# Attention, low-rank mixing and a split FFN on one core: tiles of 384 tokens from batch 2 on, short transfer latencies in the planned order, and batch 1 computed the early way

## Chip, cores and metric

The kernel runs on one core of a Trainium2 chip. The metric is the device time of one launch in microseconds (us). The core has five engines that run side by side, each taking its own instructions in order: TensorE (PE, with the loading of weights shown apart as PEld), VectorE (DVE), ScalarE (ACT), GpSimd (POOL) and SyncE (SP), which here issues the transfers between memory and on-chip buffers (DMAs).

## What is computed

There are 8 batches of 576 tokens and 8 heads of 64 channels. Each head adds two attentions: one over sequences pooled by four (144 tokens, its result repeated four times) and one over a band of seven neighbouring tokens. The result x (576 x 512 per batch) is mixed along the sequence by a product of rank 32, and then goes through an FFN of 512 to 2048 to 512 with a ReLU and a residual.

```python
q_d = q.reshape(B, H, Sd, factor, D).mean(axis=3)        # factor 4, k_d and v_d alike
out_up = np.repeat(sm_attn(q_d, k_d, v_d), factor, axis=2)
mask = np.abs(pos[:, None] - pos[None, :]) < factor
scores = np.where(mask, scale * np.matmul(q, k.transpose(0, 1, 3, 2)), -1e9)
x = out_up + np.matmul(softmax(scores), v)               # then (B, S, H * D)
h = xt @ U @ V                                           # xt: x with tokens last, rank 32
u = x + h.transpose(0, 2, 1)
return u + np.maximum(u @ w_ch1, 0.0) @ w_ch2
```

## The kernel before

**The FFN.** Tokens are cut into 16 tiles of 288, two per batch. A tile takes 16 steps, one for each 128 of the 2048 hidden channels, so there are 256 steps. A step is `ffn1` (12 matmuls at L902 into one bank `ps_h`) and, three steps later (LAG), `ffn2` (12 matmuls at L926 into four banks `acc`). The products are made of three matmuls each, since every operand is split into a high and a low part: uH and uL, hH and hL, and the two parts of the weights W. Between the two, ACT makes hH (L910) and DVE hL (L911) from `ps_h`. Up to step 19 (H1) `ps_h` has only one bank for `ffn1`, as the other serves the conversion of the weights, which arrive in 64 bits and are split by ACT, DVE and POOL (`convert`, its last piece on POOL at L357). After the last step of a tile POOL (L937) and DVE (L940) add u, and the tile is stored.

**The attention** goes by pairs of heads, four pairs per batch, numbered 0 to 31 here. It has two ways. The early way (pairs below NE = 4, batch 0) stays on the chip: banded scores in blocks on PE (L601), their transposes (L644) and products (L656), the pooled attention (ps_s L459, ps_t L488, ps_a L499), transposes of the outcome (L678, L679, L685), and the mixing by U (ps_hu, L697 and L699). POOL pools q and k (L428, L430) and v (L445, L448). The late way (all other pairs) makes band scores on PE (L745, L751, L758), bounces them and the results through memory (s_s, up_s, x_s), computes the band on POOL (L829), DVE (L834) and ACT, and mixes with ps_hu at L878 from xH and xL (L870 on POOL). Both ways end in `u_tail`: ps_u at L715, the sum on DVE, uH on ACT (L722), uL on POOL (L724). An FFN tile needs uH and uL of all four pairs of its batch.

**The order.** Nothing is issued in the order of the source. Every operation goes into a `Plan` with its engine, a cost, what it reads and writes and a priority; `Plan.run` is a list scheduler that lets the five engines run in modelled time and takes on each the ready operation of lowest priority value. Attention has priorities from 0 to 319 (10 per pair), the weights 30 and up, FFN steps 1000 and up, so FFN matmuls fill what attention leaves free, and the outcome is a fixed order of instructions for each engine. A matmul of the FFN costs PH or PF in the plan. A transfer costs its bytes plus a latency, and late transfers (priority from 50, and again from 80) a surcharge of 1.5 to 4 us (L262), so their readers are put later in the order. The buffers of the late way are opened (`open_late`) when all early work is done. Attention of batch b + 1 enters the plan with the first step of batch b.

Of the kernel before, what the change touches and what calls it, by code (L numbers as in the profile page):

```python
# [200 lines left out]
def attn_mix_ffn_kernel(ctx: ExitStack, tc, q, kp, vp, qT, kT, v, U, Ub, V, w1, w2, edge, band, eye, pool, vw, ident, outT):  # L201
# [507 lines left out]
    def u_tail(b, hp, stk, lt, xT, bank, prio):  # L709
        for t in range(NT):  # L710
            tsl = slice(t * TN, (t + 1) * TN)
# [2 lines left out]
            def um(tsl=tsl, pu=pu):
                nc.tensor.matmul(pu()[:, :TN], lt(), Vst[:, tsl], start=True, stop=True)  # L715
            op(PE, 0.14, um, [(stk, 0), (stk, 1), (stk, 2), "V0H", "V1H", "V0L", "V1L"], [pu], prio)
# [2 lines left out]
            dve(TN, lambda pu=pu, uf=uf: nc.vector.tensor_tensor(
                out=uf(), in0=pu()[:, :TN], in1=uf(), op=ALU.add), [pu, ufk], [ufk], prio)  # L720
            uH, uL = u_of(b, t)
            act(TN, lambda uH=uH, uf=uf: nc.scalar.activation(uH()[:, hp, :], uf(), AF.Copy),  # L722
                [ufk], [(uH, hp)], prio, 0.1)
            pool_tt(TN, lambda uH=uH, uL=uL, uf=uf: nc.gpsimd.tensor_tensor(  # L724
                out=uL()[:, hp, :], in0=uf(), in1=uH()[:, hp, :].bitcast(F32), op=ALU.subtract),
                [ufk, (uH, hp)], [(uL, hp)], prio)
# [114 lines left out]
    def u_of(b, t):
        if (b, t) not in u_bufs:
            u_bufs[(b, t)] = (buf(ffn, [128, NDC, TN], F32R, "uH", bufs=2), buf(ffn, [128, NDC, TN], F32R, "uL", bufs=2))
        return u_bufs[(b, t)]
# [211 lines left out]
```

## Time and profile before

| what | us |
|---|---|
| median of 3 runs (lowest, highest) | 1018.7 (1018.46, 1018.81) |
| the profiled execution | 1018.72 |
| its span, first to last instruction | 1016.9 |
| first FFN matmul starts | 62.56 |
| last piece of FFN matmuls ends | 1012.11 |

The span is what the profiler saw of the core; the 1.8 us around it belong to the launch. Busy time is given by engine; a PE that is busy has an instruction in it, at whichever clock was granted. A row of the timeline gives the start, the length, the engine, the line, the tile written and those read, the shapes (contraction x weight columns, then output partitions x columns), how many instructions are drawn together, and in brackets the idle time ahead of them with what ended it. Lengths of neighbouring matmuls overlap, so what one costs is read from start to start. Rows of POOL are rough.

### The profile page before, as it was taken

The numbers are of one execution on the slowest core, as the hardware profiler recorded it, in microseconds if no ns is written. First come the engines' busy times: TensorE is split into PE (matmuls) and PEld (weight loads), VectorE is DVE, ScalarE is ACT, GpSimd is POOL, SyncE is SP. The second block draws the span as 40 slices with busy tenths as digits, with TensorE's granted clock in tenths as the row PEclk, the third lists the DMA queues.
The fourth block names the chain that finished last, engine by engine and source line by source line (L and its number), as shares of the span: only waits on it lengthen the run. The fifth ranks groups of instructions, "written<-read, shape, count | busy, mean of one in ns | idle before, by whom it ended". The sixth has DMA issues, their size and how long they took to land.

```text
span 1016.9 us, 26970 instructions
## 1 busy us (share of the span) xinstructions
PE 981.1 (96%) x10820; PEld 962.4 (95%) x10820; DVE 471.1 (46%) x945; ACT 387.5 (38%) x1239; POOL 578.6 (57%) x651
## 2 busy tenths in 40 slices
PE   5889899999999999999999999999999999999998
PEld 4679789989999999999999999999999999999998
DVE  5788864534544445454443445445443344221111
ACT  4866644433343342443443333333433232111110
POOL 6667897867565557675756657476675543211010
PEclk9979999999999999999999999999999999999999
DMA  9677955646364465564455553446555241000000
GB/s 262 196 233 210 278 132 125 169 100 148 81 148 106 120 134 138 119 142 106 106 144 123 139 122 92 114 101 159 132 130 122 65 99 53 8 6 19 6 20 24
DMA packets 222981, 120.23 MB, mean 118 GB/s; under 512 B 174772, under 2 KB 199176, under 8 KB 222856
## 3 DMA queue, kind: packets, MB, share of 16 engines
q1 hardware_dynamic: 222856, 118.51, 46.2%
q8 instruction: 85, 1.39, 0.6%
q14 instruction: 40, 0.33, 0.1%
HBM read 87.60 MB, written 30.86 MB: 116 GB/s over the span
## 4 chain that ended last, share of the span: by engine, by line
PE 87%; DMA 3%; POOL 3%; ACT 3%; DVE 2%; issue 1%; SPq 1%; POOLq 0%; ACTq 0%; DVEq 0%
PE ps_h L902 37%; PE acc L926 37%; PE ps_a L564 3%; PE ps_b L745 2%; PE ps_hu L878 2%; PE ps_t L551 1%; DMA vr<-in_v 1%; PE ps_b L758 1%; DMA gT<-in_kT 1%; POOL Pt L829 1%; PE ps_u L715 1%; POOL W L357 1%; PE ps_a L499 1%; DMA wr<-in_W 0%; DMA xL<-x_s 0%
## 5 line engine op out<-in xcount | busy, mean ns | idle before, releaser
L926 PE MATMUL acc<-hH,W 128*128 128x288 f32 x2048 | 463.1, 299 | 3.0 <-POOL W L357 3.0
L902 PE MATMUL ps_h<-uH,W 128*128 128x288 f32 x2048 | 455.5, 297 | 6.3 <-DVE hL L911 5.9
L902 PEld LDWEIGHTS ps_h<-uH,W 128*128 128x128 f32 x2048 | 345.6, 189 | 8.3 <-DVE hL L911 7.4
L926 PEld LDWEIGHTS acc<-hH,W 128*128 128x128 f32 x2048 | 344.3, 188 | 5.1 <-POOL W L357 4.1
L902 PE MATMUL ps_h<-uL,W 128*128 128x288 f32 x1024 | 304.0, 297 | 2.2 <-POOL uL L724 2.2
L911 DVE SCALAR_TENSOR_TENSOR hL<-ps_h,hH 128x288 fp32r<-128x288 f32 x256 | 116.7, 456 | 400.6 <-ACT hH L910 400.0
L926 PE MATMUL acc<-hL,W 128*128 128x288 f32 x1024 | 301.2, 294 | 0.0
L829 POOL TENSOR_TENSOR Pt<-vl,at 128x896 f32<-128x896 f32 (+1 forms) x140 | 242.5, 1808 | 56.4 <-DVE acc L834 49.9
L910 ACT ACTIVATE hH<-ps_h 128x288 fp32r<-128x288 f32 x256 | 105.1, 410 | 440.2 <-PE ps_h L902 440.1
L902 PEld LDWEIGHTS ps_h<-uL,W 128*128 128x128 f32 x1024 | 193.9, 189 | 2.4 <-POOL uL L724 2.4
L926 PEld LDWEIGHTS acc<-hL,W 128*128 128x128 f32 x1024 | 192.9, 188 | 0.0
L834 DVE TENSOR_REDUCE acc<-Pt 128x128 f32<-128x1024 f32 (+1 forms) x140 | 150.9, 1104 | 9.4 <-POOL Pt L829 4.8
L870 POOL TENSOR_TENSOR xL<-xL,xH 116x640 fp32r<-116x640 f32 x28 | 44.0, 1571 | 91.5 <-ACT xH L869 82.0
L724 POOL TENSOR_TENSOR uL<-xT,uH 128x288 fp32r<-128x288 f32 x64 | 50.2, 808 | 70.2 <-ACT uH L722 70.1
L937 POOL TENSOR_TENSOR o<-uH,uL 128x288 f32<-128x288 f32 x64 | 49.7, 811 | 55.1 <-DMA out_t<-o 55.1
L776 ACT ACTIVATE se<-ps_b 96x114 f32<-96x114 f32 x112 | 40.0, 357 | 57.1 <-PE ps_b L751 35.6
L823 ACT ACTIVATE Pt<-ul 128x128 f32<-128x128 f32 (+1 forms) x140 | 49.8, 442 | 21.6 <-DVE acc L834 17.6
L522 POOL TENSOR_TENSOR vr<-vr 72x256 f32<-72x256 f32 x56 | 41.4, 740 | 23.7 <-DMA vr<-in_v 23.7
L357 POOL TENSOR_TENSOR W<-c,W 128x512 fp32r<-128x512 f32 x32 | 41.3, 1292 | 13.1 <-ACT W L354 12.8
L537 ACT ACTIVATE E<-ps_b,nb 72x144 f32<-72x144 f32 x112 | 40.9, 373 | 0.6
L532 DVE TENSOR_REDUCE mx<-ps_b 72x2 f32<-72x288 f32 x56 | 23.1, 448 | 35.4 <-ACT se L776 32.9
L940 DVE TENSOR_TENSOR o<-acc,o 128x288 f32<-128x288 f32 x64 | 26.6, 452 | 24.3 <-PE acc L926 21.9
(134 smaller groups left out, 894.6 us busy)
## 6 DMA issues: line engine op xcount, KB each, us to landing
wr<-in_W SPq DMA_DIRECT2D x32, 512.0 KB
vl<-in_vp SPq DMA_DIRECT2D x56, 240.0 KB
vr<-in_v SPq DMA_DIRECT2D x64, 144.0 KB
out_t<-o SPq DMA_DIRECT2D x64, 144.0 KB
gT<-in_kT SPq DMA_DIRECT2D x28, 291.0 KB
gq<-in_qT SPq DMA_DIRECT2D x28, 288.0 KB
up_s<-od SPq DMA_DIRECT2D x112, 72.0 KB
ul<-up_s SPq DMA_DIRECT2D x28, 288.0 KB
```

What stands on the lines that cost most here:

```text
L357: pool_tt(1.0 * n, lambda: nc.gpsimd.tensor_tensor(out=lo_out(), in0=ta()[l0:], in1=hi_out()[l0:].bitcast(F32), op=ALU.subtract), [t, *own ...
L522: pool_tt(256, lambda x=x: nc.gpsimd.tensor_tensor(out=x()[:, :, 0:2, :], in0=x()[:, :, 0:2, :], in1=x()[:, :, 2:4, :], op=ALU.add), [x], ...
L724: pool_tt(TN, lambda uH=uH, uL=uL, uf=uf: nc.gpsimd.tensor_tensor(out=uL()[:, hp, :], in0=uf(), in1=uH()[:, hp, :].bitcast(F32), op=ALU.su ...
L823: act(n * D, lambda n=n, ps=ps, Pt=Pt: nc.scalar.activation(Pt()[:, :n, :, 7], ul()[:, ps, :], AF.Copy), [ul], [(Pt, 1)], prio, 0.16)
L829: nc.gpsimd.tensor_tensor(out=Pt()[:, :n, :, 0:7].rearrange("p s d o -> p o s d"), in0=win, in1=at()[:, ps, :].rearrange("p s o -> p o s") ...
L834: dve(8.5 * n * D, lambda n=n, ps=ps, Pt=Pt: nc.vector.tensor_reduce(out=acc()[:, ps, :], in_=Pt()[:, :n], axis=AX.X, op=ALU.add), [(Pt, 0 ...
L870: pool_tt(640, lambda: nc.gpsimd.tensor_tensor(out=xL(), in0=xL().bitcast(F32), in1=xH().bitcast(F32), op=ALU.subtract), [xL, xH], [xL], prio)
L902: nc.tensor.matmul(ps()[:, :TN], W1[fc]()[:, w, dc, :], u()[:, dc, :], start=(n == 0), stop=(n == 3 * NDC - 1))
L910: last_h[i] = act(TN, lambda: nc.scalar.activation(hH(), ps()[:, :TN], AF.Relu), [ps], [hH], FIRST, 0.05)
L911: dve(TN, lambda: nc.vector.scalar_tensor_tensor(hL(), ps()[:, :TN], 0.0, hH().bitcast(F32), op0=ALU.max, op1=ALU.subtract), [ps, hH], [hL ...
L926: nc.tensor.matmul(ac[e]()[:, :TN], W2[fc]()[:, w, es], hx(), start=(fc == 0 and n == 0), stop=(fc == NFC - 1 and n == 2))
L937: pool_tt(TN, lambda e=e, o1=o1: nc.gpsimd.tensor_tensor(out=o1()[:, :TN], in0=uH()[:, e, :].bitcast(F32), in1=uL()[:, e, :].bitcast(F32), ...
```

## The change

1. **Tiles.** The first two batches keep tiles of 288 tokens; the other six batches, 3456 tokens, are cut into 9 tiles of 384, which cross borders of batches. A list `tiles` holds start and width, `segs` for every batch which part of which tile it fills, and `u_tail` writes one part after the other. There are 13 tiles and 208 steps. uH and uL of a wide tile lie in two buffers (a class `Half`: three of four groups of channels together, the fourth in a ring `u3`). The sum at the end of a tile uses one buffer `o`, which shares its slot with the conversion's scratch.
2. **Early way for batch 1.** NE goes from 4 to 8, so pairs 4 to 7 go the early way and enter the plan ahead of the weights. v of these pairs is loaded and pooled head by head (two smaller sums on POOL per head).
3. **Order.** The surcharge on late transfers falls to 0.25 us from priority 50 and 0.5 from 80. PE's cost in the plan follows the width. U for the late way (`load_u`) is loaded between the weights.
4. **Room.** Pt has two buffers instead of three, od two instead of three, at is written over ms, xH and Y share a slot.

```diff
-    TN = 288
+    TN, TW = 288, 384
...
-    PH, PF = 1.587, 0.398
+    PE_N = lambda n, k: k * (n / 2400.0 + 0.0125)
...
+    UC = 10
...
-    NE = 4
-    NOD = 3
+    NE = 8
+    NOD = 2
...
-        late = (3.0 if r else 4.0) * (0.5 * (prio >= 50) + 0.5 * (prio >= 80))
+        late = 0.25 * (prio >= 50) + 0.25 * (prio >= 80)
...
-        x = (buf(early_pool, [QH, 2, 2, 4, D], F32, "vr") if b else
-             buf(wts, [QH, 2, 2, 4, D], F32, "vr", f"W2_{NFC - 6 - hp}:vr"))
...
+        both = None if b else buf(wts, [QH, 2, 2, 4, D], F32, "vr", f"W2_{NFC - 6 - hp}:vr")
+        for hh in range(2):
+            x = both or buf(early_pool, [QH, 2, 4, D], F32, "vr")
...
+            pool_tt(256, lambda xh=xh: nc.gpsimd.tensor_tensor(
+                out=xh()[:, :, 0:2, :], in0=xh()[:, :, 0:2, :], in1=xh()[:, :, 2:4, :], op=ALU.add),
+                [(x, hh)], [(x, hh)], prio)
+            pool_tt(128, lambda hh=hh, xh=xh: nc.gpsimd.tensor_tensor(
...
-        ms, mx = lb([128, NPOS, 7], "ms"), lb([128, NPOS], "lmx")
+        ms, mx = lb([128, NPOS, 7], "ms", bufs=2), lb([128, NPOS], "lmx")
...
-        at = lb([128, NPOS, 7], "at", bufs=2)
+        at = ms
...
-            Pt = buf(loc, [128, 2, D, 8], F32, "Pt", "Pt", 3)
+            Pt = buf(loc, [128, 2, D, 8], F32, "Pt", "Pt", 2)
...
+    tiles, segs = [], {}
+    for g0 in (*range(0, NB * S, TN), *range(NB * S, B * S, TW)):
+        n = TN if g0 < NB * S else TW
+        for b in range(g0 // S, (g0 + n - 1) // S + 1):
+            lo, hi = max(g0, b * S), min(g0 + n, (b + 1) * S)
+            segs.setdefault(b, []).append((len(tiles), slice(lo - b * S, hi - b * S), slice(lo - g0, hi - g0)))
+        tiles.append((g0, n))
...
-        xH = buf(mix, [MP, 2, MJ, D], F32R, "xH")
+        xH = buf(mix, [MP, 2, MJ, D], F32R, "xH", "xH:x")
...
-        Y = buf(mix, [128, S // 32, 32], F32, "Y")
+        Y = buf(mix, [128, S // 32, 32], F32, "Y", "xH:y")
...
-                    nc.tensor.matmul(ps()[:, :TN], W1[fc]()[:, w, dc, :], u()[:, dc, :],
+                    nc.tensor.matmul(ps()[:, :tn], W1[fc]()[:, w, dc, :], u.ap(dc),
...
-        mm_op[i] = op(PE, PH, mm, ur + [(W1[fc], "H"), (W1[fc], "L")], [ps], FILL + i,
+        mm_op[i] = op(PE, PE_N(tn, 3 * NDC), mm, ur + [(W1[fc], "H"), (W1[fc], "L")], [ps], FILL + i,
...
-    steps = [(b, t, fc) for b in range(B) for t in range(NT) for fc in range(NFC)]
+    steps = [(ti, fc) for ti in range(len(tiles)) for fc in range(NFC)]
...
     attention(0)
+    attention(1)
     early_ops = [o for o in plan.ops if o not in tails]
...
+        if c == UC:
+            load_u(W1P + WS * (2 * c - 1))
...
-    load_u(36)
...
-    attention(1)
+    opener = {segs[b][0][0] * NFC: b + 1 for b in range(1, B - 1)}
     for i in range(len(steps) + LAG):
         if i < len(steps):
-            b, t, fc = steps[i]
-            if t == 0 and fc == 0 and b > 0 and b + 1 < B:
-                attention(b + 1)
+            if i in opener:
+                attention(opener[i])
             ffn1(steps[i], i)
```

What this does to the order shows at three places. In the rows, L numbers are lines of the program before or after it; L902 and L926 became L939 and L964, L715 became L721, L724 became L730.

PE, the last pair ahead of the first FFN matmul (W_0 and W_1 are the first hidden chunks' weights); before:

```order
L678 MATMUL ps_c<-ident_sb,od_e_105 128x72 x2
L679 MATMUL ps_c<-ident_sb,ob 128x64
L685 MATMUL ps_x<-ident_sb,ob 128x128 x4
L697 MATMUL ps_hu<-ob,Ublk 64x128 x5
L699 MATMUL ps_hu<-od_e_105,Upool 64x128 x2
L715 MATMUL ps_u<-Vst,stk 128x288 x2
L902 MATMUL ps_h<-uH,W_0_409 128x288
L902 MATMUL ps_h<-uL,W_0_409 128x288
```

and now:

```order
L685 MATMUL ps_c<-ident_sb,ob 128x64
L691 MATMUL ps_x<-ident_sb,ob 128x128 x4
L703 MATMUL ps_hu<-ob,Ublk 64x128 x5
L705 MATMUL ps_hu<-od_e_106,Upool 64x128 x2
L494 MATMUL ps_t<-ident_sb,E_e_95 72x72 x4
L721 MATMUL ps_u<-Vst,stk 128x288 x2
L505 MATMUL ps_a<-vs_e_91,E_e_95 72x64 x4
L494 MATMUL ps_t<-ident_sb,E_e_96 72x72 x4
L505 MATMUL ps_a<-vs_e_91,E_e_96 72x64 x4
L939 MATMUL ps_h<-uH,W_0_406 128x288
L939 MATMUL ps_h<-uL,W_0_406 128x288
```

The second ps_t, ps_a, ps_t and ps_a are those of pair 4, batch 1; one ps_s of it stands a few rows further ahead. After the first two steps come the band scores; before, those of late pairs:

```order
L926 MATMUL acc_1225<-hH,W_0_959 128x288
L926 MATMUL acc_1225<-hL,W_0_959 128x288
L926 MATMUL acc_1225<-hH,W_0_959 128x288
L758 MATMUL ps_b<-smk,smq 32x144 x4
L758 MATMUL ps_b<-smk,smq 8x144 x2
L745 MATMUL ps_b<-gT,gq 32x38 x8
L751 LDWEIGHTS edge
L751 MATMUL ps_b<-edge 32x38
```

and now those of an early pair, whose 36 block matmuls (L607, L601 before) stand together:

```order
L964 MATMUL acc_1268<-hH,W_0_995 128x288
L964 MATMUL acc_1268<-hL,W_0_995 128x288
L964 MATMUL acc_1268<-hH,W_0_995 128x288
L619 LDWEIGHTS eye_sb
L619 MATMUL ps_b<-band_sb,eye_sb 128x190
L619 LDWEIGHTS eye_sb
L619 MATMUL ps_b<-band_sb,eye_sb 128x190
L607 MATMUL ps_b<-kd,qt 32x38 x36
L939 MATMUL ps_h<-uH,W_2_607 128x288
```

PE at the start of tile 2, the first of batch 1 (W_0 again, step 32); before, the end of step 31, the mixing of pair 7 and its ps_u stand directly ahead of it:

```order
L926 MATMUL acc_2486<-hH,W_15_2383 128x288
L926 MATMUL acc_2486<-hL,W_15_2383 128x288
L926 MATMUL acc_2486<-hH,W_15_2383 128x288
L878 MATMUL ps_hu<-xH,Ust 64x128 x5
L878 MATMUL ps_hu<-xL,Ust 64x128 x5
L715 MATMUL ps_u<-Vst,stk 128x288 x2
L902 MATMUL ps_h<-uH,W_0_409 128x288
L902 MATMUL ps_h<-uL,W_0_409 128x288
L902 MATMUL ps_h<-uH,W_0_409 128x288 x2
```

and now the last ps_hu and ps_u of pair 7 stand around the `ffn1` of step 29 (W_13), and step 30 (W_14) and others follow ahead of step 32:

```order
L964 MATMUL acc_2391<-hH,W_10_1899 128x288
L703 MATMUL ps_hu<-ob,Ublk 64x128 x5
L705 MATMUL ps_hu<-od_e_106,Upool 64x128 x2
L939 MATMUL ps_h<-uH,W_13_1772 128x288
L939 MATMUL ps_h<-uL,W_13_1772 128x288
```

```order
L939 MATMUL ps_h<-uL,W_13_1772 128x288
L939 MATMUL ps_h<-uH,W_13_1772 128x288
L721 MATMUL ps_u<-Vst,stk 128x288 x2
L964 MATMUL acc_2373<-hH,W_11_1994 128x288
L964 MATMUL acc_2373<-hL,W_11_1994 128x288
L964 MATMUL acc_2373<-hH,W_11_1994 128x288
```

Pair 7's last link has moved three steps ahead of the tile that needs it.

POOL ahead of the last uL of batch 0 (the second row of uL from the end in each piece is pair 2, the last pair 3; gh, smq and smk are the pooled q and k, vr and vs_e the pooled v, W the conversion); before:

```order
L724 TENSOR_TENSOR uL<-xT,uH 128x288 x2
L357 TENSOR_TENSOR W_4_904<-c_753,W_4_904 128x512
L634 TENSOR_TENSOR ms_b_100<-ms_b_100,ri_b 128x10x38
L357 TENSOR_TENSOR W_0_959<-c_765,W_0_959 128x512
L724 TENSOR_TENSOR uL<-xT,uH 128x288 x2
L357 TENSOR_TENSOR W_5_1054<-c_822,W_5_1054 128x512
L357 TENSOR_TENSOR W_1_1063<-c_938,W_1_1063 128x512
L357 TENSOR_TENSOR W_6_1085<-c_1005,W_6_1085 128x512
L357 TENSOR_TENSOR W_2_1111<-c_1077,W_2_1111 128x512
L724 TENSOR_TENSOR uL<-xT,uH 128x288 x2
```

and now:

```order
L433 TENSOR_TENSOR gh<-kd 128x288
L362 TENSOR_TENSOR W_0_995<-conv,W_0_995 128x512
L362 TENSOR_TENSOR W_5_1000<-conv,W_5_1000 128x512
L451 TENSOR_TENSOR vr<-vr 72x2x128
L730 TENSOR_TENSOR uL<-xT,uH 128x288 x2
L454 TENSOR_TENSOR vs_e_91<-vr 72x2x64
L435 TENSOR_TENSOR smk<-gh 128x144
L362 TENSOR_TENSOR W_1_1097<-conv,W_1_1097 128x512
L362 TENSOR_TENSOR W_6_1143<-conv,W_6_1143 128x512
L451 TENSOR_TENSOR vr<-vr 72x2x128
L362 TENSOR_TENSOR W_2_1172<-conv,W_2_1172 128x512
L730 TENSOR_TENSOR uL<-xT,uH 128x288 x2
```

Poolings of batch 1 now stand among the pieces of the conversion.

More of the change, by code (lines that the diff above doesn't have):

```diff
@@ L304, in attn_mix_ffn_kernel @@
     kept = {}
-    count = {"y": 0}
+    count = {"y": 0, "c": 0}
+    conv = buf(ffn, [128, 3 * CN], I32, "conv", "cT:c", 1)
     def ring(shape, name, n=2, eng=None):
@@ L709, in u_tail, with um @@
     def u_tail(b, hp, stk, lt, xT, bank, prio):
[L710 to L711 removed]
+        for t, (ti, tsl, us) in enumerate(segs[b]):
+            n = tsl.stop - tsl.start
             pu = bank("ps_u", 1 - t)
[L714 to L716 removed]
+            def um(n=n, tsl=tsl, pu=pu):
+                nc.tensor.matmul(pu()[:, :n], lt(), Vst[:, tsl], start=True, stop=True)
+            op(PE, PE_N(n, 1), um, [(stk, 0), (stk, 1), (stk, 2), "V0H", "V1H", "V0L", "V1L"], [pu], prio)
             n0 = len(plan.ops)
             uf, ufk = (lambda tsl=tsl: xT()[:, tsl]), (xT, t)
[L719 to L726, printed above, removed]
+            dve(n, lambda n=n, pu=pu, uf=uf: nc.vector.tensor_tensor(
+                out=uf(), in0=pu()[:, :n], in1=uf(), op=ALU.add), [pu, ufk], [ufk], prio)
+            uH, uL = u_of(ti)
+            act(n, lambda uH=uH, uf=uf, us=us: nc.scalar.activation(uH.ap(hp, us), uf(), AF.Copy),
+                [ufk], [uH.key(hp, b)], prio, 0.1)
+            pool_tt(n, lambda uH=uH, uL=uL, uf=uf, us=us: nc.gpsimd.tensor_tensor(
+                out=uL.ap(hp, us), in0=uf(), in1=uH.ap(hp, us).bitcast(F32), op=ALU.subtract),
+                [ufk, uH.key(hp, b)], [uL.key(hp, b)], prio)
             tails.update(plan.ops[n0:])
@@ L837, in local_attn, with __init__, ap, key @@
             [(acc, p) for p in range(0, NPOS, 2)], [(x_s, 0), (x_s, 1)], prio)
-    u_bufs = {}
[L841 to L844, printed above, removed]
+    tiles, segs = [], {}
[5 more added lines that the diff above has]
+        tiles.append((g0, n))
+    u_bufs = {}
+    class Half:
+        def __init__(self, ti, name):
+            n = tiles[ti][1]
+            if n == TN:
+                w = buf(ffn, [128, NDC, TN], F32R, name, bufs=2)
+                self.parts = [(w, dc) for dc in range(NDC)]
+            else:
+                w = buf(ffn, [128, NDC - 1, TW], F32R, name, bufs=2)
+                x = buf(loc, [128, TW], F32R, "u3", "u3", 4)
+                self.parts = [(w, dc) for dc in range(NDC - 1)] + [(x, None)]
+            self.ti, self.n = ti, n
+        def ap(self, dc, c=slice(None)):
+            x, k = self.parts[dc]
+            a = x()[:, 0:self.n] if k is None else x()[:, k, :]
+            return a[:, c]
+        def key(self, dc, b):
+            return (self.parts[dc][0], dc, b)
+        def keys(self, dc):
+            return [self.key(dc, b) for b in range(B) for t, _, _ in segs[b] if t == self.ti]
+    def u_of(ti):
+        if ti not in u_bufs:
+            u_bufs[ti] = (Half(ti, "uH"), Half(ti, "uL"))
+        return u_bufs[ti]
     def mix_part(b, hp, x_s, prio):
         xL = buf(mix, [MP, 2, MJ, D], F32R, "xL")
-        xH = buf(mix, [MP, 2, MJ, D], F32R, "xH")
+        xH = buf(mix, [MP, 2, MJ, D], F32R, "xH", "xH:x")
         def load():
@@ L893, in ffn1 @@
     def ffn1(s, i):
-        b, t, fc = s
-        uH, uL = u_of(b, t)
+        ti, fc = s
+        tn = tiles[ti][1]
+        uH, uL = u_of(ti)
         ps = psum(ps_h, "ps_h", f"h{i % 2 * (i >= H1):d}:f", 1)
```

71 lines of the change are left out of this document (35 added, 36 removed).

## Prediction

> **What bounds the kernel now.** I read the page's head, the busy time by stage, the chain of work that ended last, the waits of PE, and then single stretches of the timeline.
>
> ```profile
> span 1016.9 us, 26970 instructions
> PE 981.1 (96%) x10820; PEld 962.4 (95%) x10820; DVE 471.1 (46%) x945; ACT 387.5 (38%) x1239; POOL 578.6 (57%) x651
> PE 87%; DMA 3%; POOL 3%; ACT 3%; DVE 2%; issue 1%; SPq 1%; POOLq 0%; ACTq 0%; DVEq 0%
> ```
>
> PE is busy for 96% of the span and makes up 87% of the chain, so time is what PE has to do plus what it waits. The next rows give, for each stretch, its length and the busy time (and count) of PE, its weight loads, DVE, ACT and POOL, then the granted clock, the DMA share and GB/s.
>
> ```profile
> 0.00:62.50 62.50, 43.32 (x868) 35.48 (x869) 44.39 (x108) 39.40 (x125) 39.82 (x58) 0.96 0.75 223
> 62.50:130.00 67.50, 60.91 (x731) 58.18 (x730) 56.75 (x104) 44.87 (x125) 53.86 (x60) 0.94 0.86 247
> 130.00:200.00 70.00, 67.40 (x812) 65.82 (x810) 37.89 (x77) 30.57 (x103) 57.53 (x62) 1.00 0.58 136
> 200.00:214.00 14.00, 10.35 (x72) 9.79 (x72) 8.64 (x15) 4.53 (x14) 12.17 (x16) 0.88 0.46 125
> ...
> 250.00:850.00 600.00, 599.82 (x6645) 594.56 (x6645) 276.47 (x541) 228.80 (x760) 373.43 (x410) 1.00 0.49 117
> ```
>
> There are two regimes. From 250 to 850 us PE is never idle, and only fewer or shorter PE instructions can save time. From 62.5 to 200 us it stands still for 67.50 - 60.91 + 70.00 - 67.40 = 9.2 us, and new PE work placed there can cost less than its length. The waits of PE in 62.5 to 214 us (sum, times, longest), and the one row of 250 to 850 us, say why:
>
> ```profile
> PE ps_h L902 <- DVE hL L911: 5.9, 6, 1.7
> PE acc L926 <- POOL W L357: 3.0, 5, 1.2
> PE ps_hu L878 <- ACT E L537: 0.2, 1, 0.2
> ```
>
> **The change part by part.** *Wider tiles.* 16 tiles of 288 tokens make 256 steps of 24 matmuls, 6144 in all. After it, 4 tiles of 288 and 9 of 384 make 208 steps: 1536 matmuls of 288 columns and 3456 of 384, in all the same number of columns. The price of 288 columns stands in the chain near the end, where nothing else runs on PE; that of 128 columns in a stretch of the timeline with ten matmuls of one kind; that at half the clock at the first FFN matmuls.
>
> ```profile
> 954.28 1.60 PE acc L926 x12
> ...
> 973.41 1.60 PE acc L926 x12
> ```
> ```profile
> 256.85 0.47 PE L878 MATMUL ps_hu<-xH,Ust 116*64 116x128 f32 x5
> 257.15 0.47 PE L878 MATMUL ps_hu<-xL,Ust 116*64 116x128 f32 x5
> 257.45 0.35 PE L926 MATMUL acc<-hH,W 128*128 128x288 f32 x1
> ```
> ```profile
> 62.56 0.45 PE L902 MATMUL ps_h<-uH,W 128*128 128x288 f32 x1
> 62.80 0.45 PE L902 MATMUL ps_h<-uL,W 128*128 128x288 f32 x1
> ```
>
> Between the first two rows lie twelve pieces of 12 matmuls: 19.13 us / 144 = 132.8 ns each. Ten of 128 columns take 257.45 - 256.85 = 0.60 us, 60 ns each. At half clock 288 columns take 240 ns, exactly twice 120. So at full clock something is added to 120 ns for 288 columns (12.8) and to 53.3 for 128 columns (6.7): about in proportion to the columns, a line of 0.453 ns per column plus 2.5 ns. On that line 384 columns take 176.4 ns. The ends: if the added 12.8 ns were the same for every width, 172.8 ns; if all of it went with the columns, 177.1. The sum before is 6144 x 132.8 = 815.9 us; after, 204.0 + 3456 x 176.4 = 813.6. **FFN: -2.3 us** (ends -14.7 and 0). I take the line, since the constant misses the 128 columns by 6 ns and finds nothing at half clock.
>
> A rule of the Trainium skill bears on this ("TensorE: Matmul & The Clock Gate", section "Wait — 56ns, not 53.3ns?"): a warm matmul follows the one before it after N/2.4 ns plus a fixed 2.5 ns, a cold one after exactly N/1.2. The trace agrees when cold and not when warm, where 288 columns take 10.3 ns longer than the rule. By its fixed part, an estimate, 1152 fewer matmuls save 2.9 us; it speaks against a large gain from wider tiles.
>
> *Batch 1 the early way.* The price of an early pair comes from the timeline before the FFN; the profile counts each f32 matmul that is not a transpose twice, so x72 are the 36 of one pair.
>
> ```profile
> 42.45 0.32 PE L613 MATMUL ps_b<-band_sb,eye_sb 128*128 128x190 bf16 x2
> 42.71 0.84 PE L601 MATMUL ps_b<-kd,qt 64*32 64x38 f32 x72
> 43.48 0.73 PE L499 MATMUL ps_a<-vs_e,E_e 128*72 128x64 f32 x8
> 44.14 1.04 PE L656 MATMUL ps_ba<-vw,et 38*32 38x64 f32 x80
> 45.11 0.71 PE L459 MATMUL ps_s<-smk,smq 64*72 64x144 f32 x8
> ...
> 46.27 0.66 PE L685 MATMUL ps_x<-ident_sb,ob 128*128 128x128 f32 x4
> 47.59 1.31 PE L697 MATMUL ps_hu<-ob,Ublk 128*64 128x128 f32 x10 [0.66 <-DVE xT L688]
> ...
> 49.27 0.44 PE L488 MATMUL ps_t<-ident_sb,E_e 72*72 72x72 f32 x4
> 50.49 0.73 PE L499 MATMUL ps_a<-vs_e,E_e 128*72 128x64 f32 x8 [0.79 <-ACT E_e L492]
> 51.04 0.51 PE L715 MATMUL ps_u<-Vst,stk 128*128 128x288 f32 x2
> 51.39 0.41 PE L488 MATMUL ps_t<-ident_sb,E_e 72*72 72x72 f32 x4
> 51.64 0.60 PE L644 MATMUL ps_bt<-ident_sb,ms_b 128*128 128x128 f32 x4
> ```
>
> From start to start: block scores 1.03, ps_a 0.66 twice, ps_ba 0.97, ps_s and the ps_c behind it 1.16, ps_x 0.5 (its 0.66 less the overlapping end), ps_hu 1.68, ps_t 0.25 twice, ps_u 0.35, ps_bt 0.7 for five. Together 8.2 us. A late pair is what remains of 250 to 850 us beside the FFN; these rows are the stretch for L902, L926 and L715 alone:
>
> ```profile
> 250.00:850.00 600.00, 285.01 (x1943) 266.21 (x1943) 1.00 0.49 117
> 250.00:850.00 600.00, 294.46 (x1944) 267.27 (x1944) 1.00 0.49 117
> 250.00:850.00 600.00, 9.05 (x42) 6.71 (x42) 1.00 0.49 117
> ```
>
> Two ps_u per pair make 21 pairs: (600 - 3887 x 0.1328) / 21 = 4.0 us. So the early way costs PE 4.2 us more per pair, 16.8 for four. Of these, ps_s (0.7), both ps_t and both ps_a of pair 4 (2.5 us) stand ahead of the first FFN matmul, where PE works 43.32 of 62.50 us. **Early pairs: +14.4 us** of PE work behind that point (12 if re-entries into the FFN are cheaper than in the late pairs, 17 if dearer).
>
> *Tile 2's start.* Here the last late pair of batch 1 stood directly ahead of step 32.
>
> ```profile
> 199.18 0.46 PE L878 MATMUL ps_hu<-xH,Ust 116*64 116x128 f32 x5
> 200.00 0.51 PE L878 MATMUL ps_hu<-xL,Ust 116*64 116x128 f32 x5 [0.36 <-POOL xL L870]
> 201.55 0.50 PE L715 MATMUL ps_u<-Vst,stk 128*128 128x288 f32 x2 [1.04 <-DVE stk L883]
> 203.69 0.40 PE L902 MATMUL ps_h<-uH,W 128*128 128x288 f32 x1 [0.44 <-ACT uH L722]
> 206.26 0.40 PE L902 MATMUL ps_h<-uL,W 128*128 128x288 f32 x1 [2.17 <-POOL uL L724]
> ```
>
> The four waits named are 4.0 us; the half clock behind them costs 1.7 (0.12 of the 14.0 us of this stretch, whose mean clock is 0.88). In the new order ps_u of pair 7 comes right behind the ffn1 of step 29, with five pieces of 1.6 us between it and step 32, so uH and uL have about 8 us. **-5.7 us** (ends 0 and -6).
>
> *Idle of 62.5 to 200 us.* Of the 9.2 us the new work can fill some. Up to step 16 the two orders give PE about equal insert work (one early pair's rest and parts of two, against scores, ps_t and ps_a of three late ones) and DVE, 84% busy there, the same; after it PE has more and POOL and DVE less, as no local attention runs before the early work is done. I take half, **-4.6 us**; ends 0 and -9.2.
>
> *Start of the FFN.* PE has 2.5 us more ahead of it, and POOL the poolings of pairs 4 and 5 (L433, L435) and the split sums of vr (L451, L454) ahead of the last uL. Both engines have 19 to 23 us free there. **+1 us**, from -3 (PE denser, so full clock from 62.56 on) to +5 (all of it in the chain).
>
> *The rest.*
>
> ```profile
> L829 POOL TENSOR_TENSOR Pt<-vl,at 128x896 f32<-128x896 f32 (+1 forms) x140 | 242.5, 1808 | 56.4 <-DVE acc L834 49.9
> L834 DVE TENSOR_REDUCE acc<-Pt 128x128 f32<-128x1024 f32 (+1 forms) x140 | 150.9, 1104 | 9.4 <-POOL Pt L829 4.8
> ```
>
> The last tile's adds and stores are a third wider: +0.5. At nothing: Pt with two buffers (POOL's product takes 1808 ns, DVE's sum 1104, so POOL still sets the pace), the shared slots of at, xH/Y and o (16 steps or a whole pair lie between uses), wider hL and uL (DVE 46%, POOL 62% in the steady part), and the short latencies in the plan; if that cover is gone, PE waits, which is the second rival.
>
> **Sum** against the profiled execution (1018.72 us: the span and 1.8 us outside it, 0.02 from the median): -2.3 + 14.4 - 5.7 - 4.6 + 1 + 0.5 = +3.3, so **1022.0 us**.
>
> **Rivals.** *The added time is per matmul* (384 columns in 172.8 ns): -12.4 us more, 1009.6. For it: 12.8 and 6.7 ns belong to matmuls of different height and weight width. Against: the 6.7 itself, and no such addition at half clock. Chance 0.22.
>
> *Short latencies make PE wait* (the slower side beyond the forecast). The plan now adds 0.25 or 0.5 us to late transfers where it added 1.5 to 4. Each late pair comes back to PE with ps_b, ps_t, ps_a, ps_hu and ps_u; an instruction placed before its data stops the FFN matmuls queued behind it, and hH, hL with them. It decides once a transfer lands later than the plan's move and fixed time plus 0.5 us. At 0.5 us a pair, 24 pairs, +12: 1034. Against it: in 600 us PE now waits 0.2 us in all, so there is slack to spend. Chance 0.15.
>
> *The early stage fills all its holes*: 9.2 instead of 4.6 us of idle, and full clock from the start, -4 against my +1: 1022.0 - 4.6 - 4 = 1013.4. Against it: DVE is 84% busy there and hL is what PE waits for most. Chance 0.13.
>
> **How the numbers follow.** The forecast has 0.50, with its own range of 1017 to 1029 from the ends of its terms. A measurement of this kernel tells about 0.2%, 2 us, from no change. Slower: 0.37 of the forecast and 0.15 of the latencies, 0.52. Same: 0.13 and 0.02, 0.15. Faster: 0.22 and 0.11, 0.33. The range, 1009 to 1031, takes in the per-matmul case and most of the ends; what lies beyond is mostly the latencies.
>
> **What will show it.** Twelve matmuls of 384 columns in the chain: 2.12 us on the line, 2.07 if constant. The first FFN matmul between 60 and 68 us. No stall near 200 us ahead of step 32. Four early pairs near 8 us of PE each. Waits of PE beyond 250 us under 1 us; a list of waits on xL, E or gT there would be the second rival. The forecast is wrong if 384 columns take under 174 ns, or if PE's idle between FFN start and step 32 falls below 2 us.

## The result, and the profile after

The changed kernel took 1029.69 us (median of 4 runs, 1028.43 to 1034.3), the one before 1018.66 (1018.46 to 1018.81): ratio 1.012 (95% interval 1.010 to 1.0139), 11 us slower. It lies inside the range of the prediction and on the side it forecast, but 7.7 us above the forecast of 1022.0. The profiled execution took 1028.43 us, its span is 1026.3.

From the page of the changed kernel, the span, the busy time by engine and the chain by engine:

```profile
span 1026.3 us, 25019 instructions
PE 993.8 (97%) x9980; PEld 965.0 (94%) x9980; DVE 450.6 (44%) x885; ACT 378.7 (37%) x1171; POOL 536.0 (52%) x618
PE 71%; DMA 8%; POOL 7%; SPq 4%; ACT 3%; DVE 3%; issue 3%; DVEq 0%; ACTq 0%; POOLq 0%
```

PE's share of the chain fell from 87% to 71%; DMA and POOL took over, so at places PE now runs only when a transfer or POOL's work is done. The shares are not the length of its waits: PE is idle for 32.5 us in all, 16.8 of them ahead of the first FFN matmul. The stretches of the changed kernel (length, busy time of PE, PEld, DVE, ACT, POOL, clock, DMA share, GB/s) say where:

```profile
0.00:66.60 66.60, 49.81 (x900) 40.83 (x901) 47.37 (x114) 42.81 (x140) 47.99 (x78) 0.95 0.82 247
66.60:129.00 62.40, 60.96 (x669) 58.35 (x668) 55.12 (x110) 40.66 (x98) 41.96 (x47) 0.97 0.54 184
129.00:199.60 70.60, 70.60 (x905) 67.48 (x904) 20.16 (x54) 20.30 (x62) 13.54 (x18) 1.00 0.14 41
328.80:746.00 417.20, 409.76 (x4330) 399.17 (x4329) 203.52 (x372) 176.02 (x585) 293.32 (x326) 0.99 0.58 138
746.00:951.00 205.00, 205.00 (x1215) 204.81 (x1214) 49.86 (x90) 36.50 (x84) 45.25 (x44) 1.00 0.11 29
```

From 66.6 to 199.6 us PE is idle for 1.4 us where it was idle for 9.2. POOL has almost nothing to do from 129 to 199.6 (13.54 of 70.6 us), as the late way is not open yet. Then nearly all the work of the 24 late pairs stands between 200 and 746 us, and from 328.8 us on PE is idle there for 7.4 us. PE's waits from 200 to 900 us, where before there was 0.2 us behind tile 2's start, are many and small (sum, times, longest):

```profile
PE ps_u L721 <- DVE stk L919: 3.0, 3, 2.3
PE ps_t L557 <- ACT E L543: 1.7, 3, 1.1
PE ps_b L764 <- POOL smk L435: 1.3, 3, 0.6
PE ps_hu L914 <- ACT E L543: 0.9, 1, 0.9
...
PE ps_a L570 <- POOL vs L530: 0.8, 1, 0.8
```

They stand at every link of a late pair: the pooled k and v (smk, vs), the softmax (E) and the mixed result (stk). Near the end, where PE has only the FFN, the chain gives the price of 384 columns:

```profile
930.84 2.09 PE ps_h L939 x12
...
1014.30 2.09 PE ps_h L939 x12
1016.39 4.70 PE acc L964 x27
```

Between the first and the last row are 41 pieces of 12: 85.55 us / 492 = 173.9 ns, where the prediction had 176.4 and its rival 172.8.

Where the time went can be added up from the starts and ends of PE's instructions: each FFN matmul is charged 132.8 or 173.9 ns, the time in which PE runs nothing is idle, what FFN matmuls took beyond that is half clock and re-entry after inserts, and the rest are inserts (attention).

| part of the span (us) | before | after | difference | prediction |
|---|---|---|---|---|
| first FFN matmul at | 62.56 | 66.62 | +4.1 | +1 |
| FFN matmuls | 815.8 | 804.8 | -11.0 | -2.3 |
| inserts | 102.8 | 118.3 | +15.5 | +14.4 |
| tiles 0 to 2: idle, half clock and re-entry | 12.9 + 10.6 | 2.9 + 6.5 | -14.1 | -10.3 |
| tile 3 on: idle | 0.2 | 9.2 | +9.0 | 0 |
| tile 3 on: half clock and re-entry | 8.2 | 14.0 | +5.8 | 0 |
| behind the last FFN start | 3.9 | 4.0 | +0.1 | +0.5 |
| span | 1016.9 | 1026.3 | +9.4 | +3.3 |

### The profile page after: what moved, and what is told of

Its sections match the earlier page's. It is cut to its first block, busy times and chain, and to the rows that moved or that the text cites. A ratio compares the mean times of both kernels' runs of the same rounds, so it can differ in the third digit from the quotient of the medians.

```text
span 1026.3 us, 25019 instructions
## 1 busy us (share of the span) xinstructions
PE 993.8 (97%) x9980; PEld 965.0 (94%) x9980; DVE 450.6 (44%) x885; ACT 378.7 (37%) x1171; POOL 536.0 (52%) x618
## 4 chain that ended last, share of the span: by engine, by line
PE 71%; DMA 8%; POOL 7%; SPq 4%; ACT 3%; DVE 3%; issue 3%; DVEq 0%; ACTq 0%; POOLq 0%
PE ps_h L939 30%; PE acc L964 29%; POOL Pt L835 4%; DMA ul<-up_s 2%; DMA vr<-in_v 2%; PE ps_a L570 2%; PE ps_b L751 1%; DVE acc L840 1%; DMA Y<-x_s 1%; PE ps_hu L703 1%; PE ps_a L505 1%; PE ps_hu L914 1%; SPq L790 1%; SPq L579 1%; PE ps_u L721 1%
## 5 line engine op out<-in xcount | busy, mean ns | idle before, releaser
L964 PE MATMUL acc<-hH,W 128*128 128x384 f32 (+1 forms) x1664 | 445.6, 328 | 0.0
L939 PE MATMUL ps_h<-uH,W 128*128 128x384 f32 (+1 forms) x1376 | 359.2, 323 | 1.4 <-DVE hL L948 1.4
L964 PEld LDWEIGHTS acc<-hH,W 128*128 128x128 f32 x1664 | 297.6, 188 | 1.9 <-ACT hH L947 0.4
L964 PE MATMUL acc<-hL,W 128*128 128x384 f32 (+1 forms) x832 | 268.6, 323 | 0.0
L948 DVE SCALAR_TENSOR_TENSOR hL<-ps_h,hH 128x384 fp32r<-128x384 f32 (+1 forms) x208 | 109.0, 524 | 343.5 <-ACT hH L947 343.3
L939 PEld LDWEIGHTS ps_h<-uH,W 128*128 128x128 f32 x1376 | 246.0, 189 | 2.5 <-DVE hL L948 2.0
L947 ACT ACTIVATE hH<-ps_h 128x384 fp32r<-128x384 f32 (+1 forms) x208 | 97.2, 468 | 343.6 <-PE ps_h L939 340.2
L939 PE MATMUL ps_h<-uL,W 128*128 128x384 f32 (+1 forms) x688 | 221.3, 322 | 0.0
L835 POOL TENSOR_TENSOR Pt<-vl,ms 128x896 f32<-128x896 f32 (+1 forms) x120 | 204.6, 1793 | 31.3 <-DMA vl<-in_vp 20.1
L964 PEld LDWEIGHTS acc<-hL,W 128*128 128x128 f32 x832 | 156.5, 188 | 0.0
L939 PEld LDWEIGHTS ps_h<-uL,W 128*128 128x128 f32 x688 | 130.3, 189 | 0.0
L730 POOL TENSOR_TENSOR uL<-xT,uH 128x384 fp32r<-128x384 f32 (+2 forms) x52 | 41.1, 809 | 125.4 <-ACT uH L728 125.4
L939 PE MATMUL ps_h<-u,W 128*128 128x384 f32 x432 | 100.1, 340 | 0.0
L939 PEld LDWEIGHTS ps_h<-u,W 128*128 128x128 f32 x432 | 77.9, 188 | 0.0
```

Source lines behind the costliest of these rows:

```text
L730: pool_tt(n, lambda uH=uH, uL=uL, uf=uf, us=us: nc.gpsimd.tensor_tensor(out=uL.ap(hp, us), in0=uf(), in1=uH.ap(hp, us).bitcast(F32), op=AL ...
L835: nc.gpsimd.tensor_tensor(out=Pt()[:, :n, :, 0:7].rearrange("p s d o -> p o s d"), in0=win, in1=at()[:, ps, :].rearrange("p s o -> p o s") ...
L939: nc.tensor.matmul(ps()[:, :tn], W1[fc]()[:, w, dc, :], u.ap(dc), start=(n == 0), stop=(n == 3 * NDC - 1))
L947: last_h[i] = act(tn, lambda: nc.scalar.activation(hH()[:, :tn], ps()[:, :tn], AF.Relu), [ps], [hH], FIRST, 0.05)
L948: dve(tn, lambda: nc.vector.scalar_tensor_tensor(hL()[:, :tn], ps()[:, :tn], 0.0, hH()[:, :tn].bitcast(F32), op0=ALU.max, op1=ALU.subtract ...
L964: nc.tensor.matmul(ac[e]()[:, :tn], W2[fc]()[:, w, es], hx()[:, :tn], start=(fc == 0 and n == 0), stop=(fc == NFC - 1 and n == 2))
```

## The experiments

The open question is the row of tile 3 and later. Below, "idle from tile 3 on" is PE's idle time from the first matmul of tile 3 to the last steps, from one stretch of each kernel's profile. That is one execution each, and not always one near the median.

### Is it the short latencies? (A), or the crowding of the late pairs? (B)

Four kernels. The old surcharge in the changed kernel:

```diff
-        late = 0.25 * (prio >= 50) + 0.25 * (prio >= 80)
+        late = (3.0 if r else 4.0) * (0.5 * (prio >= 50) + 0.5 * (prio >= 80))
```

> The changed kernel with the old surcharge of 1.5 to 4 us on late transfers. Theory A (the plan's short latencies make PE wait): the 8.4 us that PE stands idle from tile 3 to the end, and some 3 us of half clock and restarts around it, go; 1017 to 1020 us, idle from tile 3 on under 1.5 us. Theory B (24 late pairs crowded into 550 us, because they start only at 200 us, make transfers and engines late, whatever the plan believes): 1027 to 1031 us, idle from tile 3 on still 6 us or more.

The reverse of that line in the kernel before:

> The kernel before with the new surcharge of 0.25 and 0.5 us and nothing else. Theory A: 28 late pairs wait as the 24 do in the changed kernel; 8 to 14 us slower than before, 1026 to 1033 us, idle of PE from tile 3 on 7 us or more (0.2 before). Theory B: 1017 to 1021 us, idle from tile 3 on under 2 us.

The changed kernel with batch 1 late again:

```diff
-    NE = 8
+    NE = 4
...
     attention(0)
-    attention(1)
     early_ops = [o for o in plan.ops if o not in tails]
...
+    attention(1)
     opener = {segs[b][0][0] * NFC: b + 1 for b in range(1, B - 1)}
```

> The changed kernel with batch 1 computed the late way again (NE 4), wide tiles and short latencies kept. By theory A the waits from tile 3 on stay, and what goes is the early pairs' price, net: the start 4 us earlier and 15.5 us less insert work, against some 14 us of idle and half clock that come back in tiles 0 to 2: about 1024 us (1020 to 1028). By theory B the late pairs begin at 65 us and have room: waits from tile 3 on under 2 us, 1010 to 1015 us.

And both of these edits:

> The changed kernel with NE 4 and the old surcharge, so the wide tiles and the smaller buffers alone. Both theories: the wide matmuls at 173.9 ns give 11 us, 1007 to 1010 us, faster than before. If the smaller buffers (Pt 2, at over ms, xH and Y in one slot) cost something, it stands above 1011 us. Theory A has it 10 us or more under the same kernel with short latencies; theory B within 3 us of it.

| kernel | median us (range) | ratio to before (interval) | idle from tile 3 on |
|---|---|---|---|
| changed, old surcharge | 1051.18 (1050.88 to 1052.72) | 1.0323 (1.0305 to 1.0340) | 26.3 |
| before, short latencies | 1018.9 (1017.68 to 1020.88) | 1.0004 (0.9993 to 1.0015) | 1.5 |
| changed, NE 4 | 1019.62 (1015.11 to 1025.45) | 1.0017 (0.9997 to 1.0036) | 5.0 |
| changed, NE 4, old surcharge | 1050.0 (1048.2 to 1051.64) | 1.0308 (1.0288 to 1.0328) | 24.2 |

Neither theory stands. Short latencies alone cost nothing, so A as I put it falls. Without the early way for batch 1 (NE 4) 10 of the 11 us are gone, and the idle time is 5.0 us instead of 9.2, which lies between the two theories. With the old surcharge the wide kernel loses 21 us with NE 8 and 30 with NE 4, which no theory had. The timeline of the changed kernel with the old surcharge shows most of that loss at one place (in brackets the idle time ahead), and the row of the stretch, with 18.6 of the 26.3 us of idle time, its effect on the clock (0.87):

```profile
424.65 1.41 PE L557 MATMUL ps_t<-ident_sb,E 72*72 72x72 f32 x8 [3.45 <-ACT E L543]
436.15 0.79 PE L914 MATMUL ps_hu<-xH,Ust 116*64 116x128 f32 x5 [10.09 <-ACT xH L905]
437.77 0.80 PE L914 MATMUL ps_hu<-xL,Ust 116*64 116x128 f32 x5 [0.82 <-POOL xL L906]
440.16 0.87 PE L721 MATMUL ps_u<-Vst,stk 128*128 128x192 f32 x2 [1.60 <-DVE stk L919]
```
```profile
335.00:441.00 106.00, 87.36 (x855) 84.09 (x844) 42.76 (x77) 39.30 (x127) 64.70 (x72) 0.87 0.49 113
```

That ps_u is pair 15's, the last of batch 3, and behind it stands step 80, the first of tile 5. Tile 5 is the first that crosses a border: 192 tokens of batch 2 and 192 of batch 3. So batch 3's four pairs are due half a wide tile sooner, at about 420 us, where in the kernel before batch 3's first tile began at 443. In both kernels these pairs come to their ps_u after batch 2's first step. From there they had two tiles before (step 64 at 322 us to step 96 at 443) and have one now (step 64 at 329 to step 80 at 420); batch 4 then has two wide tiles again (420 to 580). With the old surcharge the pairs come some 25 us apart (ps_u of pair 8 at 262 us, of pair 15 at 440) and miss that date.

### Is it the crossing? (C), or the late start of the late way? (D)

All tiles of 288 tokens, with the changed kernel's other parts, with short latencies and with the old surcharge:

```diff
-    for g0 in (*range(0, NB * S, TN), *range(NB * S, B * S, TW)):
-        n = TN if g0 < NB * S else TW
+    for g0 in range(0, B * S, TN):
+        n = TN
```

> The changed kernel with all tiles of 288 tokens (early way for batch 1, short latencies and the smaller buffers kept), so no tile crosses a border of batches. Theory C (a tile of 384 that crosses a border needs the next batch's attention half a tile sooner; the late pairs are pressed together and PE waits): idle of PE from tile 3 on under 2 us, and what is left against the kernel before is the early way alone, 4 us of later start and 15.5 us of inserts less 14 us of idle and half clock in tiles 0 to 2: 1022 to 1026 us. Theory D (the waits come from the late way's start at 200 us, whatever the tiles): idle from tile 3 on 5 us or more, and the 11 us of narrower matmuls on top: 1035 to 1041 us.

> As the one before with the old surcharge on late transfers: the early way for batch 1 and the smaller buffers alone. Theory C: without crossing tiles the surcharge matters little, 1021 to 1027 us, no single wait above 3 us behind tile 2 (10.1 us in the changed kernel with the old surcharge). Theory D: the late start leaves too little time, 1035 us or more.

Wide tiles that don't cross, 384 and 192 tokens in each batch, again with both surcharges:

```diff
-    for g0 in (*range(0, NB * S, TN), *range(NB * S, B * S, TW)):
-        n = TN if g0 < NB * S else TW
+    cuts = [(g, TN) for g in range(0, NB * S, TN)] + [c for b in range(NB, B) for c in ((b * S, TW), (b * S + TW, S - TW))]
+    for g0, n in cuts:
...
```

> The changed kernel with each of batches 2 to 7 cut into a tile of 384 and one of 192 tokens, so wide tiles without crossing. 2304 matmuls of 384 columns and 2304 of 192: by a line through 288 and 384 columns (132.8 and 173.9 ns) 192 take 91.7 ns, by the line of the prediction 89.5, by a constant of 12.8 ns 92.8; FFN about 8 us more than in the changed kernel. Theory C: idle from tile 3 on under 3 us, 1022 to 1028 us. Theory D: idle as in the changed kernel, 1036 to 1040 us.

> As the one before with the old surcharge. Theory C: the stall of about 20 us ahead of step 80 that the changed kernel showed with this surcharge is gone, 1021 to 1029 us. Theory D, or a surcharge that is bad for itself: 1045 us or more.

| kernel | median us (range) | ratio to before (interval) | idle from tile 3 on |
|---|---|---|---|
| 288, short | 1039.51 (1038.16 to 1040.45) | 1.0215 (1.0188 to 1.0242) | 12.6 |
| 288, old surcharge | 1021.9 (1021.28 to 1024.66) | 1.0041 (1.002 to 1.0062) | 4.3 |
| 384 and 192, short | 1076.57 (1075.02 to 1078.88) | 1.0589 (1.0561 to 1.0618) | 3.0 |
| 384 and 192, old surcharge | 1075.08 (1073.85 to 1076.64) | 1.0568 (1.0544 to 1.0592) | 3.9 |

For the stall C is right: with the old surcharge and no crossing, nothing stands ahead of step 80, in either shape of tile. For the small waits it is wrong: 288 tokens and short latencies have 12.6 us of them without any crossing tile. The old surcharge with 288 tokens leaves the early way and the smaller buffers alone: 4 us slower than before.

The kernels with 192 tokens came out 46 us and more above what theory C gave, and not by waiting. In the chain of the kernel with short latencies:

```profile
1032.33 1.34 PE ps_h L939 x12
...
1056.45 1.34 PE ps_h L939 x12
1057.79 1.34 PE acc L964 x12
```

From the first to the last row are 19 pieces of 12: 25.46 us / 228 = 111.7 ns for a matmul of 192 columns. On the prediction's line it would be 89.5. So 2304 of these matmuls took 46 us more than the 91.7 ns that I had put. Something other than columns holds a narrow matmul, and its weights of 128 columns are the candidate: the ten matmuls of 128 columns that the prediction used, 60 ns each, have weights of 64. The changed kernel's trace has four others of 128 columns, with weights of 128, at a clock of 1.00:

```profile
164.78 0.60 PE L691 MATMUL ps_x<-ident_sb,ob 128*128 128x128 f32 x4
```

They start 108 ns apart (the 0.60 us less the 0.27 that the last one takes, by three). And where a single ps_u of 192 columns, with weights of 128, stands directly ahead of a wider one, the next one starts 88 to 90 ns after it in ten of eleven places of that trace (166 ns in the one behind the wait of 2.3 us). So 192 columns are not slow by themselves; many in a row are, each with a new weight load. The Trainium skill ("TensorE: Matmul & The Clock Gate", section "LDWEIGHTS (loading the stationary operand)") gives a weight load its columns over 1.2, in ns, so by an estimate from it 106.7 ns for 128 columns and 53.3 for 64; the 111.7 and 108 ns of the traces are 5.0 and 1.3 ns above it, which agrees. The 60 ns are 6.7 above it, but they are as far above the 53.3 ns that the prediction had for 128 columns of data, so they tell nothing of which limit held them. No run here changed the width of the weights alone, and the ps_x are transposes, not products.

### What turns short latencies into waits?

288 tokens, NE 4, short latencies: beside the kernel before with short latencies the smaller buffers are left, with the small edits that go with them (the sums of v in two parts, U's place in the order, PE's cost in the plan).

> The changed kernel with tiles of 288 tokens and batch 1 the late way, short latencies and smaller buffers kept; beside the kernel before with short latencies alone (1018.9 us, PE idle 1.6 us from tile 3 on) only the buffers differ, beside the changed kernel with 288 tokens (1039.5 us, idle 12.6) only the early way of batch 1. Theory D2 (short latencies turn into waits where the late pairs must catch up, because the early way holds them back to 200 us): idle from tile 3 on under 3 us. Theory F (the smaller buffers make PE wait under short latencies): 8 us or more. For the stage before tile 3: if the shared scratch and the split sums of v cost the early stage its 8 us (kernel with NE 4: tile 0 in 78.9 us, before 70.1), tile 0 takes 77 us or more here too; 1024 to 1030 us by D2, 1032 or more by F.

A surcharge between, with the changed kernel otherwise as it is:

```diff
-        late = 0.25 * (prio >= 50) + 0.25 * (prio >= 80)
+        late = 1.0 * (prio >= 50) + 1.0 * (prio >= 80)
```

> The changed kernel with a surcharge of 1 and 2 us, between its own (0.25 and 0.5) and the old one (1.5 or 2, and 3 or 4). If the surcharge trades small waits against the stall ahead of step 80: idle from tile 3 on outside that stall falls from 9.2 to 3 to 6 us, and the stall is between 2.3 and 18.6 us; 1027 to 1040 us. If the small waits do not hang on the surcharge: they stay at 8 to 10 us and the stall comes on top, 1035 or more.

NE 4 with the buffers of the early stage as they were:

```diff
-    NE = 8
-    NOD = 2
+    NE = 4
+    NOD = 3
...
-    conv = buf(ffn, [128, 3 * CN], I32, "conv", "cT:c", 1)
...
+        t = buf(ffn, [128, CN], I32, name, "cT:" + name, 3)
...
-        both = None if b else buf(wts, [QH, 2, 2, 4, D], F32, "vr", f"W2_{NFC - 6 - hp}:vr")
+        x = (buf(early_pool, [QH, 2, 2, 4, D], F32, "vr") if b else
...
```

> The changed kernel with NE 4 and, back as they were, the conversion scratch in a ring of three with the output tiles in it, v loaded and summed by pairs, three od buffers and U loaded at its old place; wide tiles, short latencies, Pt 2, at over ms and xH/Y in one slot stay. Beside the kernel with NE 4 alone (1019.6 us, step 48 at 272 us) this tells what the early buffers cost. If they do: step 48 near 263 us, and 1009 to 1013 us, faster than before. If tile 0 was slow for another reason: step 48 near 272 us, 1018 to 1021 us.

And, on top of it, xH and Y in slots of their own. To make room for them ms has one buffer, hH three, and all output tiles go through one ring of three:

```diff
-        ms, mx = lb([128, NPOS, 7], "ms", bufs=2), lb([128, NPOS], "lmx")
+        ms, mx = lb([128, NPOS, 7], "ms", bufs=1), lb([128, NPOS], "lmx")
...
-        xH = buf(mix, [MP, 2, MJ, D], F32R, "xH", "xH:x")
+        xH = buf(mix, [MP, 2, MJ, D], F32R, "xH")
...
-        Y = buf(mix, [128, S // 32, 32], F32, "Y", "xH:y")
+        Y = buf(mix, [128, S // 32, 32], F32, "Y")
...
-        hH = buf(ffn, [128, TW], F32R, "hH", bufs=4)
+        hH = buf(ffn, [128, TW], F32R, "hH", bufs=3)
...
```

> The kernel with NE 4 and the old early buffers (1022.6 us, PE idle 11.2 us from tile 3 on), with xH and Y in slots of their own again; to make room hH has three buffers, ms one, and all output tiles go through the ring of three. Short latencies, wide crossing tiles, Pt 2 and at over ms stay. Theory G (the slot shared by xH and Y is what turns short latencies into waits: the order then holds the last links of a batch's pairs back and sends them in a burst): idle from tile 3 on under 4 us, 1010 to 1015 us, faster than before by about the 11 us of the wide matmuls less some 5 us of inserts, restarts and the early crossing. If the other small buffers or the wide tiles' pace are the cause: idle stays at 8 us or more, 1019 to 1025 us.

| kernel | median us (range) | ratio to before (interval) | idle from tile 3 on |
|---|---|---|---|
| 288, NE 4, short | 1044.04 (1039.8 to 1051.5) | 1.0243 (1.0215 to 1.027) | 20.0 |
| changed, surcharge 1 and 2 us | 1027.73 (1025.85 to 1030.29) | 1.0098 (1.0077 to 1.0119) | 9.5 |
| NE 4, old early buffers | 1022.62 (1021.84 to 1024.09) | 1.0048 (1.0033 to 1.0063) | 11.2 |
| the same, own slots | 1021.14 (1018.15 to 1024.92) | 1.0023 (1.0003 to 1.0042) | 5.6 |

The first of these decides between the late start and the smaller buffers: without the early way there are more waits, not fewer, so the late start is not their cause. The rows of the two kernels with short latencies, 288 tokens and NE 4, from tile 3 on; first with the old buffers, then with the smaller ones:

```profile
263.70:1010.00 746.30, 744.83 (x7618) 738.34 (x7617) 296.43 (x589) 241.88 (x789) 379.61 (x421) 1.00 0.39 94
```
```profile
269.80:1040.00 770.20, 750.21 (x7610) 740.84 (x7609) 295.88 (x589) 244.04 (x790) 375.71 (x417) 0.99 0.40 91
```

The engines do the same work (POOL 380 and 376 us, DVE 296), and PE stands still for 1.5 and 20.0 us. The second profile is of the slowest of four executions, 1051.5 us, so at the median the waits may be fewer. It waits, in the second, at each kind of link:

```profile
PE ps_a L570 <- POOL vs L530: 5.4, 6, 1.5
PE ps_b L764 <- DVE od L574: 4.0, 2, 2.3
PE ps_b L764 <- POOL smk L435: 2.5, 1, 2.5
PE ps_hu L914 <- ACT E L543: 2.0, 2, 1.5
```

The surcharge of 1 and 2 us shows that the waits also hang on the plan's latencies: in that kernel PE waits for nothing at all from 423 us, the start of tile 5, to the end. All its 9.5 us stand ahead of step 80, half of them in one wait of the pair that is due there:

```profile
PE ps_hu L914 <- ACT xH L905: 4.7, 1, 4.7
PE ps_a L570 <- POOL vs L530: 2.6, 1, 2.6
PE ps_u L721 <- DVE stk L919: 1.0, 1, 1.0
```

So the surcharge trades the small waits everywhere against one stall at the first crossing: 2.3 us at the most with 0.25 and 0.5, 4.7 with 1 and 2, 10.1 with the old one, and the sum hardly moves between the first two (1029.7 and 1027.7, intervals of the ratio 1.010 to 1.0139 and 1.0077 to 1.0119).

The last two kernels ask which of the smaller buffers. With the old early buffers, step 48 comes at 266.5 us instead of 272.1, and tile 0 takes 69.1 us instead of 78.9 (70.1 in the kernel before, 76.0 with 288 tokens and NE 4), so the shared scratch, the split sums, od with two buffers or U's place (not tried apart) did cost the early stage; but its waits from tile 3 on are 11.2 us and the median is not better. Giving xH and Y their own slots halves the waits, between what the two theories said.

The times at which the four pairs of a batch come to their ps_u (us, from the traces) show what this slot does to the order:

| kernel | batch 4 | batch 5 | pause between |
|---|---|---|---|
| before, short latencies | 416, 448, 484, 503 | 526, 566, 615, 637 | 23 |
| 288, old surcharge | 465, 495, 521, 551 | 580, 610, 638, 666 | 29 |
| 288, short | 469, 482, 500, 514 | 600, 616, 629, 642 | 86 |
| 288, NE 4, short | 476, 490, 503, 521 | 608, 623, 636, 660 | 87 |
| changed | 444, 463, 493, 512 | 589, 603, 616, 630 | 77 |
| NE 4, old early buffers | 428, 450, 471, 494 | 589, 602, 617, 630 | 94 |
| the same, own slots | 421, 438, 461, 484 | 507, 566, 621, 638 | 23 |

With the shared slot and short latencies together the pairs of a batch come in a burst, and then none for 77 to 94 us. With either of the two taken back (the slot with the small changes beside it) the pause is 23 to 29 us, close to the spacing within a batch (41 and 52 us in the two wide kernels with the old surcharge). The burst is not the whole of the waits: the kernel of 384 and 192 tokens with short latencies has a pause of 85 us too, and with its longer FFN PE is idle for 3.0 us only.

Part of what is left in the last kernel, 1.4 us, comes from the ring of three for the output tiles, which also holds up the last tile's sums; a row of PE's waits and one of the timeline's end:

```profile
PE acc L960 <- DVE o L974: 1.4, 2, 1.2
```
```profile
1014.31 0.99 POOL L971 TENSOR_TENSOR o<-u,u 128x384 f32<-128x384 f32 x1 [55.77 <-DMA out_t<-o]
```

Behind the start of its last FFN matmul this kernel needs 6.0 us, 2 more than the others. No version came out faster than before; the two nearest, this one and the changed kernel with NE 4 alone (0.9997 to 1.0036), are level with it or a few tenths of a per cent slower.

## Why the prediction was right, and where it was not

**The direction and its main reason were right.** The early way's price on PE is the largest term, +14.4 forecast, and inserts rose by 15.5. Counted by lines, the four early pairs take 27.5 us behind the first FFN matmul, where four late pairs took 14.7 (102.8 / 28 x 4), so 12.8 of it are theirs, near the low end that I gave (12). The other 2.7 are the 24 late pairs, which cost 3.8 us each instead of 3.7. **Tile 2's start and the early idle** came out better than forecast: -14.1 for -10.3. The half of the early idle that I took was too little, as 7.8 of its 9.2 us went, and part of the half clock of the early stage went too. That is the third rival's mechanism, without its earlier start. **The start of the FFN**, +4.1 for +1, lies near the end of the range that I gave (+5); PE is busy for 49.8 us ahead of it instead of 43.3, POOL for 48.0 instead of 39.8. With NE 4 it starts at 62.1, so the early way's work delays it, but no run tells which engine held it.

**The FFN term was mis-sized**: -2.3 forecast, -11.0 measured, and 384 columns took 173.9 ns, under the 174 that the prediction named as its sign of being wrong. The step that failed is the line through 128 and 288 columns. The matmul of 128 columns, with weights of 64, is not of the same kind: the kernel with 192 columns shows that a stream of narrow matmuls has a price of its own, 111.7 ns with weights of 128 columns. The prediction's own row of ps_x, four matmuls of 128 columns in 0.66 us (0.13 from start to start), did not fit 60 ns each either. What is added to columns over 2.4 per ns is 12.8 ns at 288 and 13.9 at 384, all but constant, as the rival had it. The argument from half clock (nothing added there) did not carry over to full clock. The fixed 2.5 ns of the Trainium skill ("TensorE: Matmul & The Clock Gate", section "Wait — 56ns, not 53.3ns?") is 10 to 11 ns too little at either width here, and the measurement decides.

**The waits from tile 3 on were set at nothing**: they are +9.0 idle and +5.8 of half clock and re-entry, and they turn the -11.0 of the FFN and more into a loss. The step that failed is "at nothing: ... the shared slots ..., and the short latencies in the plan". The second rival named this mechanism, with +12, and 0.15; its effect is what happened, but its cause was too simple. Short latencies alone are free (ratio 1.0004), the smaller buffers with the old surcharge and the early way are nearly so (1.0041, 4.3 us of waits). With the smaller buffers and the early way, at 288 tokens, the short surcharge costs 17.6 us (1039.51 against 1021.9), and without the early way the kernel is 25 us above the one with short latencies alone (1044.04 against 1018.9). That shows the pair at work at 288 tokens; for the wide tiles, where the waits are fewer, it is argued from this and from the bursts. The forecast had also overlooked what the old surcharge would do with wide tiles: a tile of 384 that crosses a border makes the next batch due half a tile sooner, and with the old surcharge that costs 18.6 us of idle in one tile.

**Luck.** The forecast is 6.1 us from the measured spans, but its terms are further off: 8.7 too much for the FFN and 3.8 for the early stage, 14.8 too little for the waits from tile 3 on, 4.2 for the start and the inserts. They partly cancel, so the number is better than the account behind it. Two of the prediction's own signs of being wrong came true, the 173.9 ns and the 1.4 us of idle between the FFN's start and step 32 (under 2).

What stays open: how much of the waits the shared slot of xH and Y makes, and how much Pt with two buffers and at over ms. The own slots for xH and Y ended the bursts and halved the waits of one profile, but other buffers changed with them, and kernels with short latencies and smaller buffers spread by up to 12 us from run to run (1039.8 to 1051.5), so a single profile of them is no measure of a few us. Pt and at were not tried apart.

## What to carry to other kernels

A tile that crosses a border of the data moves a due date, and the cost shows only when the producers are too slow for it: look for the first step that needs the next batch, not only at the price of its matmuls. Edits that are nearly free one by one (less slack in a static order, fewer buffers) can cost 2% together, as here; cost them as a pair. Read the price of an instruction only from one of the same kind: a matmul of another width with other weights may have another limit.
